# Hash-bucketed attention and a gated MLP on one core: the row maxima's last step as one reduction, running sums on GpSimd, a new planned order

## The chip, the cores and the metric

The kernel runs on one core of one Trainium2 chip. Times are microseconds of device time for one execution. The kernel before took a median of 816.7 us in three runs (815.85 to 816.98). TensorE is the matrix engine, VectorE, ScalarE and GpSimd the three elementwise engines (DVE, ACT and POOL in the profile), SyncE (SP) issues most transfers.

## The reference

```python
def attention(q, k, v, proj):                # (4, 8, 768, 64) each, proj (64, 6)
    q_bucket = bits(q @ proj > 0)            # 6 signs make a bucket number
    k_bucket = bits(k @ proj > 0)
    mask = q_bucket[..., :, None] == k_bucket[..., None, :]
    scores = where(mask, q @ k.T / sqrt(64), -1e9)
    scores = scores - max(scores, axis=-1)
    attn = exp(scores) / (sum(exp(scores), axis=-1) + 1e-9)
    return attn @ v

def mlp(x, w_in, g_ln, w_sg, b_sg, w_out):   # x: (4, 768, 512), the 8 heads side by side
    u, v = split(gelu_tanh(x @ w_in), 2)     # 512 columns each
    v_n = (v - mean(v)) / sqrt(var(v) + 1e-6) * g_ln
    v_s = w_sg @ v_n + b_sg[:, None]         # mixes the 768 positions
    return x + (u * v_s) @ w_out
```

## The kernel before

The attention works through 16 pairs of heads (`NPAIR`), the two heads of a pair on the two halves of the 128 partitions. For precision a matrix is split into a high and a low part, and products of parts are added in PSUM.

For a pair: `load` fetches q, k and v (SP queue). `parts` transposes q and k on TensorE (L494), ScalarE writes the high part (L498), VectorE the low part (L501). `features` multiplies by the projection (L514) and VectorE turns the results into signs (L519); the signs, scaled, go into extra rows of a matmul, so that scores of unequal buckets become very negative. `largest` computes approximate scores row by row (L539), and VectorE takes their negated maxima (L547 for a row of 512 keys, L549 for the last 256 keys of two rows at once). A pair has nine such units: three for the first 256 queries (phase 0) and six for the other 512 (phase 1). After the last unit of a phase `shift` joins the two parts of the maxima: L558 takes the minimum of the negated parts, L559 replaces values of empty rows by zero and writes the result into a zeroed tile `m`; TensorE spreads `m` into rows (L565), and ScalarE copies two rows into the feature tile (L571), where they become the shift that the scores get.

`weigh` computes the shifted scores with four matmul parts (L593), ScalarE exponentiates them into a tile `p` (L598), and an add joins `p` to a running sum a head (L620). `ADDS` names the engine of each add: GpSimd for all but the third of the five in phase 1. Every three units TensorE multiplies `p` by v (L608 and L611). `finish` adds the sums over partitions (L640), sends them through DRAM to get them into another layout (L649 to L655), takes the reciprocal (L651) and multiplies (GpSimd L662, then VectorE L663) before the result is written to DRAM.

Between all this VectorE and GpSimd convert the MLP's input weights: 16 weight jobs of seven VectorE operations (L363, L364, L366, L368, L369, L370, L372), one on GpSimd (L365) and one on ScalarE (L371).

The MLP then runs over 4 batches of 768 positions. `hidden` makes both halves (L806, L834), `gate` mixes the positions (L852, then VectorE L855, L859), `project` multiplies by w_out and adds x (L878, L883). For batch 0 the mixing weights are transposed first (L772, L778, L781), and the output weights converted by eight more weight jobs.

All instructions of both parts are handed to `Plan`, each with an engine, a cost in us, a due time (`prio`), what it reads and writes, and `port=True` where it is held to exclude GpSimd from VectorE. `Plan.order` runs a list schedule with these costs: an engine takes, of what is ready in the plan, what is due first; on TensorE a change of the kind of matmul adds `STAY` to the due time. The order that comes out is the order of the program on each engine; on the chip each engine works strictly in that order and waits on semaphores. Due times are in units of half a `weigh` unit: unit g is due at 2g, its totals at 2g + `FINP`, its products at 2g + `AVP`, the maxima of unit i at 2(i - `AHEAD`) + `S0P`, the preparation of the next pair at `PREP` against its start, weight job i at `WSTEP` i + `WP`. The MLP's due times begin at 480 and so lie behind all of the attention. PSUM has 7 banks for the attention's matmuls and one for the products; 16 `p` tiles are shared.

Of the kernel before, what the change touches and what calls it, by code (L numbers as in the profile page):

```python
# [18 lines left out]
DRAM = bass.MemoryType.DRAM  # L19


MLP = {"xl": "POOL", "gm": "DVE", "gl": "POOL", "wg": 209.05, "wo": 46.93, "x": 568.79}

AVP = 4.99
GY, GX, NPT = (1, 2), (3, 3), 16
NAV = 1
S0P = 2.08
AHEAD = 8
PREP, SHIFTP, FINP, WSTEP, WP = -3.85, 0.3, 6.08, 12.04, 25.31
LOADS = "SP"  # L30
ADDS = (["POOL", "POOL"], ["POOL", "POOL", "DVE", "POOL", "POOL"])
TAILP = 0.0


class Plan:
# [8 lines left out]
    TURNS = {"row": 0.2, "col": 0.144, "full": 0.17, "c32": 0.1, None: 0.0}  # L44
    LANES = 8
    TURN = 4.7
    STAY = 2.0

    class Buf:
        def __init__(self, make, i, prev, need=None):  # L50
# [178 lines left out]
def kernel(  # L229
# [99 lines left out]
    CW = 256  # L329
    wjobs = [(w_in, c, f0, CW, wih, wil, 1.0) for f0 in range(0, FF, CW) for c in range(NC)]  # L330

    def weight_job(plan, tile_of, src, c, f0, CW, th, tl, fac, prio):
        def part(t):
            return (t() if isinstance(t, Plan.Buf) else t)[:, c, f0:f0 + CW]

        bufs = [(t, (c, f0)) for t in (th, tl) if isinstance(t, Plan.Buf)]
        w = tile_of([P, CW, 2], I32, "w64")
        x, y = tile_of([P, CW], I32, "wx"), tile_of([P, CW], I32, "wy")
        g = tile_of([P, CW], F32, "wg")
        d = plan.buf("wd", 1000)  # L340
        V = nc.vector
        sts = V.scalar_tensor_tensor

        def load():
            nc.sync.dma_start(w().rearrange("p a b -> p (a b)"), src[c * P:(c + 1) * P, f0:f0 + CW].bitcast(I32))

        ops = iter(range(1, 12))

        def when():
            i = next(ops)  # L350
            return prio

        def vec(fn, r, wr):
            plan.add("DVE", 0.07 + CW / 960.0, when(), fn, r, wr, port=True)

        def vec2(fn, r, wr):
            plan.add("DVE", 0.07 + CW / 1920.0, when(), fn, r, wr, port=True)
# [4 lines left out]
        xf, yf = (lambda: x().bitcast(F32)), (lambda: y().bitcast(F32))  # L362
        vec2(lambda: V.tensor_scalar(y(), hi(), 3, 0x3FFFFFFF, op0=ALU.logical_shift_left, op1=ALU.bitwise_and), [w], [y])  # L363
        vec(lambda: sts(x(), hi(), -0x40000000, y(), op0=ALU.bitwise_and, op1=ALU.bitwise_or), [w, y], [x])  # L364
        plan.add("POOL", 0.14 + CW / 512, when(), lambda: nc.gpsimd.tensor_mul(g(), hi().bitcast(F32), hi().bitcast(F32)), [w], [g])  # L365
        vec(lambda: sts(xf(), g(), LEAST * LEAST, xf(), op0=ALU.is_ge, op1=ALU.mult), [x, g], [x])  # L366

        vec2(lambda: V.tensor_single_scalar(y(), x(), -0x800000, op=ALU.bitwise_and), [x], [y])  # L368
        vec(lambda: sts(yf(), lo().bitcast(U32), 2.0 ** -52, yf(), op0=ALU.mult, op1=ALU.mult), [w, y], [y])  # L369
        vec(lambda: V.tensor_add(xf(), xf(), yf()), [x, y], [x])  # L370
        plan.add("ACT", 0.06 + CW / 1300, when(), lambda: nc.scalar.mul(part(th), xf(), fac), [x], [d] + bufs[:1])  # L371
        vec(lambda: sts(part(tl), xf(), fac, part(th).bitcast(F32), op0=ALU.mult, op1=ALU.subtract),  # L372
            [x, d] + bufs[:1], bufs[1:])
# [50 lines left out]
    if True:  # L424
# [82 lines left out]
        def features(st, i, prio):  # L507
            hh, lo, ft, (_, cs, keys), fp = st.hi, st.lo, st.ft, chunk(i), ps_tile()
            n = cs.stop - cs.start

            def project():
                for c, (s, _) in enumerate(keys):
                    for u, (w, x) in enumerate(((pwh, hh), (pwl, hh), (pwh, lo))):
                        nc.tensor.matmul(fp()[:, c * n:(c + 1) * n], w[:, s, :], x()[:, s, cs], start=(u == 0), stop=(u == 2))  # L514

            plan.add(PE, 0.7, prio, project, [(t, x) for t in (hh, lo, ft) for x in keys], [fp], form="full")
            for c, (s, ph) in enumerate(keys):
                def sign(c=c, s=s):
                    nc.vector.tensor_scalar(ft()[:, s, cs], fp()[:, c * n:(c + 1) * n], fcol[:, 2 * s:2 * s + 1],  # L519
                                            fcol[:, 2 * s + 1:2 * s + 2], op0=ALU.is_gt, op1=ALU.mult)  # L520

                plan.add(DVE, 0.28 + n / 960.0, prio, sign, [fp], [(ft, (s, ph))])

        def largest(st, u, prio):

            ph = 0 if u < 3 else 1
            i, w = divmod(u - 3 * ph, 3)
            if u in (0, 3):
                st.mx = late.ring([P, 2, WIDE // P, 2], F32, "mx", 3)
            mx, sc, i0 = st.mx, [ps_tile() for j in range(2)], 2 * i  # L530
            (a, b), t0 = ((0, WIDE) if w < 2 else (WIDE, S)), PHASES[ph][0] // P + i0
            tiles = (w,) if w < 2 else (0, 1)

            def mm():
                for c, t in enumerate(tiles):
                    qs = slice((t0 + t) * P, (t0 + t + 1) * P)
                    for n, x in enumerate((st.ft, st.hi)):
                        for j in range(2):
                            nc.tensor.matmul(sc[j]()[:, c * NY:c * NY + b - a], x()[row(j), 0, qs], x()[row(j), 1, a:b],  # L539
                                             start=(n == 0), stop=(n == 1))  # L540

            plan.add(PE, 0.464, prio, mm, [(x, (0, ph)) for x in (st.hi, st.ft)] + [(x, (1, c)) for x in (st.hi, st.ft) for c in ((0, 1) if w < 2 else (1,))],
                     sc, form="row")
# [29 lines left out]
        def weigh(st, c, prio):  # L573
# [22 lines left out]
            plan.add(PE, 0.93, prio, mm, [(x, (0, ph)) for x in (hi, lo, ft)] + [(x, (1, y)) for x in (hi, lo, ft) for y in need], sc, form="row")  # L596
# [4 lines left out]
            if u + 1 in ends:  # L601
# [12 lines left out]
                plan.add(PE, 0.865 * len(us), prio + AVP, product, [t for x in us for t in ps[x]] + [st.v], [av], form="col")  # L614
            if u:
                e = ADDS[ph][u - 1]
                for j in range(2):
                    def add(j=j, e=e, first=st.p[0][j] if u == 1 else sums[j]):
                        a = first()[:, :, :NY] if u == 1 else two(first())
                        (nc.gpsimd if e == POOL else nc.vector).tensor_add(two(sums[j]()), a, p[j]()[:, :, :NY])  # L620

                    plan.add(e, 1.35 if e == POOL else 0.62, prio + 0.6, add, [p[j]] + ([st.p[0][j]] if u == 1 else []),
                             [sums[j]], port=True)

        def finish(st, ph, prio):
# [31 lines left out]
            if ph == 0:  # L657
# [277 lines left out]
```

## Time and profile before

| | us |
|---|---|
| median of three runs | 816.7 |
| the profiled execution | 820.94 |
| its span, first to last instruction | 818.8 |
| TensorE busy | 782.7 (96%) |
| VectorE busy | 539.0 (66%) |
| ScalarE busy | 359.6 (44%) |
| GpSimd busy | 370.6 (45%) |
| mean granted TensorE clock | 0.987 of full |

The busy shares are means over an attention part (to some 494 us) and an MLP part. A busy TensorE is not one at its peak: matmuls overlap, and their ends are modelled. The profile's chain of waits goes through TensorE for 74% of the span and through VectorE for 19%.

### The profile page before, as it was taken

The numbers are of one execution on the slowest core, as the hardware profiler recorded it, in microseconds if no ns is written. First come the engines' busy times: TensorE is split into PE (matmuls) and PEld (weight loads), VectorE is DVE, ScalarE is ACT, GpSimd is POOL, SyncE is SP. The second block draws the span as 40 slices with busy tenths as digits, with TensorE's granted clock in tenths as the row PEclk, the third lists the DMA queues.
The fourth block names the chain that finished last, engine by engine and source line by source line (L and its number), as shares of the span: only waits on it lengthen the run. The fifth ranks groups of instructions, "written<-read, shape, count | busy, mean of one in ns | idle before, by whom it ended". The sixth has DMA issues, their size and how long they took to land.

```text
span 818.8 us, 14669 instructions
## 1 busy us (share of the span) xinstructions
PE 782.7 (96%) x5608; PEld 599.2 (73%) x5608; DVE 539.0 (66%) x962; ACT 359.6 (44%) x703; POOL 370.6 (45%) x334
## 2 busy tenths in 40 slices
PE   6999998999999899998999999999999999999998
PEld 4767566657557566665767556988899889988996
DVE  7898987997988898897678644699323141405130
ACT  2556653646546454654656574532332123213211
POOL 0376664666556464663756676344006112401030
PEclk9999998999999999999999999999999999999999
DMA  5233232232232143232230123631402220131003
GB/s 129 52 86 73 66 98 58 68 98 73 64 100 60 65 104 73 60 92 52 54 98 21 54 78 118 218 98 39 129 27 78 82 73 6 34 124 31 1 1 128
DMA packets 98533, 60.63 MB, mean 74 GB/s; under 512 B 64672, under 2 KB 85280, under 8 KB 98464
## 3 DMA queue, kind: packets, MB, share of 16 engines
q1 hardware_dynamic: 96768, 56.94, 25.0%
q10 hardware_dynamic: 1696, 2.76, 1.0%
q8 instruction: 44, 0.72, 0.4%
q14 instruction: 25, 0.20, 0.1%
HBM read 46.90 MB, written 12.78 MB: 73 GB/s over the span
## 4 chain that ended last, share of the span: by engine, by line
PE 74%; DVE 19%; DMA 2%; issue 2%; ACT 2%; SPq 0%; POOL 0%; ACTq 0%; DVEq 0%
PE g L593 14%; PE ps_vs L852 11%; PE ps_o L878 8%; PE g L539 7%; PE av L608 7%; PE ps_h L806 7%; PE ps_h L834 6%; PE g L514 4%; PE av L611 4%; PE g L494 3%; DVE m L559 3%; DVE mx L547 2%; DVE mx L549 2%; DVE mx L558 2%; DVE xt L663 1%
## 5 line engine op out<-in xcount | busy, mean ns | idle before, releaser
L598 ACT ACTIVATE p<-g 128x512 f32<-128x512 f32 x288 | 155.7, 600 | 102.5 <-PE g L593 101.7
L620 POOL TENSOR_TENSOR sum<-sum,p 128x512 f32<-128x512 f32 x128 | 159.3, 1264 | 55.9 <-DVE sum L620 32.0
L547 DVE TENSOR_REDUCE mx<-g 128x1 f32<-128x512 f32 x192 | 121.7, 679 | 21.3 <-PE g L539 18.6
L620 POOL TENSOR_TENSOR sum<-p,p 128x512 f32<-128x512 f32 x64 | 85.4, 1354 | 87.4 <-ACT p L598 87.4
L608 PE MATMUL av<-p,v 128*64 128x512 f32 x384 | 89.6, 602 | 0.0
L593 PE MATMUL g<-h 64*128 64x256 f32 (+1 forms) x384 | 76.3, 360 | 5.6 <-DVE mx L547 4.9
L549 DVE TENSOR_REDUCE mx<-g 128x2 f32<-128x512 f32 x96 | 61.9, 684 | 23.9 <-PE g L539 22.0
L539 PE MATMUL g<-f 64*128 64x256 f32 (+1 forms) x384 | 73.2, 366 | 0.8 <-DVE f L519 0.5
L855 DVE SCALAR_TENSOR_TENSOR gt<-ps_vs,g_col,b_bc 128x384 f32<-128x384 f32 x32 | 19.7, 616 | 80.3 <-PE ps_vs L852 80.3
L593 PE MATMUL g<-h,l 64*128 64x256 f32 (+1 forms) x384 | 72.1, 342 | 0.0
L593 PE MATMUL g<-l,h 64*128 64x256 f32 (+1 forms) x384 | 71.0, 339 | 0.0
L593 PE MATMUL g<-f 64*128 64x256 f32 (+1 forms) x384 | 70.9, 338 | 0.0
L539 PE MATMUL g<-h 64*128 64x256 f32 (+1 forms) x384 | 68.3, 342 | 0.0
L863 POOL TENSOR_TENSOR gs<-gt,gs 128x384 fp32r<-128x384 f32 x32 | 32.8, 1026 | 74.0 <-ACT gs L860 74.0
L878 PE MATMUL ps_o<-woh,gs 128*128 128x512 f32 x192 | 65.5, 402 | 0.0
L852 PE MATMUL ps_vs<-wgh,zh 128*128 128x384 f32 x192 | 64.3, 335 | 0.6 <-DVE gt L855 0.6
L852 PE MATMUL ps_vs<-wgh,zl 128*128 128x384 f32 x192 | 64.2, 334 | 0.0
L852 PE MATMUL ps_vs<-wgl,zh 128*128 128x384 f32 x192 | 64.2, 334 | 0.0
L817 POOL TENSOR_TENSOR mv<-mv,epsr 128x1 f32<-128x1 f32 x24 | 15.6, 651 | 100.8 <-DVE mv L816 100.8
L593 PEld LDWEIGHTS g<-h 64*128 64x128 f32 x384 | 41.4, 186 | 26.8 <-DVE mx L547 8.8
L814 DVE BATCH_NORM_STATS2 st<-y 128x6 f32<-128x512 f32 x24 | 16.6, 690 | 64.0 <-ACT y L795 64.0
L608 PEld LDWEIGHTS av<-p,v 128*64 128x64 f32 x384 | 24.9, 137 | 43.8 <-issue 41.8
(118 smaller groups left out, 1754.1 us busy)
## 6 DMA issues: line engine op xcount, KB each, us to landing
q<-in_q_dram SPq DMA_DIRECT2D x32, 192.0 KB
k<-in_k_dram SPq DMA_DIRECT2D x32, 192.0 KB
v<-in_v_dram SPq DMA_DIRECT2D x16, 384.0 KB
x<-xs SPq DMA_DIRECT2D x16, 384.0 KB
rx<-xs SPq DMA_DIRECT2D x96, 64.0 KB
out_dram<-ob SPq DMA_DIRECT2D x24, 256.0 KB
w<-in_moe_w_in_dram SPq DMA_DIRECT2D x16, 256.0 KB
rs<-r SPq DMA_DIRECT2D x32, 128.0 KB
```

What stands on the lines that cost most here:

```text
L539: nc.tensor.matmul(sc[j]()[:, c * NY:c * NY + b - a], x()[row(j), 0, qs], x()[row(j), 1, a:b], start=(n == 0), stop=(n == 1))
L547: nc.vector.tensor_reduce(mx()[:, 0, i0 + w, j:j + 1], sc[j]()[:, :WIDE], axis=AX.X, op=ALU.max, negate=True)
L549: nc.vector.tensor_reduce(mx()[:, 1, i0:i0 + 2, j], two(sc[j]()), axis=AX.X, op=ALU.max, negate=True)
L593: nc.tensor.matmul(sc[j]()[:, i * w:(i + 1) * w], x()[row(j), 1, ks], y()[row(j), 0, cs], start=(m == 0), stop=(m == 3))
L598: plan.add(ACT, 0.6, prio, lambda j=j: nc.scalar.activation(p[j]()[:, :, :NY], two(sc[j]()), AF.Exp, scale=SCALE), [sc[j]], [p[j]])
L608: nc.tensor.matmul(two(av())[row(j)], st.v()[:, j, x, :], ps[x][j]()[:, :, :NY], start=(x == 0), stop=(x == 5))
L620: (nc.gpsimd if e == POOL else nc.vector).tensor_add(two(sums[j]()), a, p[j]()[:, :, :NY])
L806: nc.tensor.matmul(ps(), x()[:, ts_], w[:, c, FH:FF], start=(c == 0 and n == 0), stop=(c == NC - 1 and n == 2))
L834: nc.tensor.matmul(ps()[:, :SH], w[:, c, fs], x()[:, cs], start=(c == 0 and n == 0), stop=(c == NC - 1 and n == 2))
L852: nc.tensor.matmul(vp(), z()[:, t, fs], w()[:, t, cs], start=(t == 0 and n == 0), stop=(t == NT - 1 and n == 2))
L863: nc.gpsimd if e == POOL else nc.vector).tensor_sub(gl()[:, cs], gt(), gh()[:, cs].bitcast(F32)),
L878: nc.tensor.matmul(po(), a()[:, ts_], w()[:, f, :], start=(f == 0 and n == 0), stop=False)
```

## The change

The two operations L558 and L559 become one tensor_reduce. The tile of the maxima gets a third part that holds the constant `EMPTY` and is set once at the start, in three fixed tiles that are used in turn; the reduction takes the minimum over the three parts and writes into `m`. A row without a match now has `EMPTY` as its shift instead of zero. The one add of a pair's phase that ran on VectorE goes to GpSimd, for both heads. Costs and due times of the plan are changed, and L663 is no longer marked as excluding GpSimd. The weight job gets a `bank` argument with a second form of its operations; the callers don't pass it.

```diff
-MLP = {"xl": "POOL", "gm": "DVE", "gl": "POOL", "wg": 209.05, "wo": 46.93, "x": 568.79}
+MLP = {"xl": "POOL", "gm": "DVE", "gl": "POOL", "wg": 105.79, "wo": 112.68, "x": 652.19}
-AVP = 4.99
+AVP = 5.2
-S0P = 2.08
+S0P = 1.57
-PREP, SHIFTP, FINP, WSTEP, WP = -3.85, 0.3, 6.08, 12.04, 25.31
+PREP, SHIFTP, FINP, WSTEP, WP = -4.32, 0.3, 2.81, 14.6, 25.31
-ADDS = (["POOL", "POOL"], ["POOL", "POOL", "DVE", "POOL", "POOL"])
-TAILP = 0.0
+ADDS = (["POOL", "POOL"], ["POOL", "POOL", "POOL", "POOL", "POOL"])
+TAILP = 1.27
+WHURRY = 20.0
...
-    STAY = 2.0
+    STAY = 2.64
...
-    def weight_job(plan, tile_of, src, c, f0, CW, th, tl, fac, prio):
+    def weight_job(plan, tile_of, src, c, f0, CW, th, tl, fac, prio, bank=None):
...
+        mxs = [late.pool.tile([P, 3, WIDE // P, 2], F32, tag=f"mx{i}", name=f"mx{i}", bufs=1) for i in range(3)]
+        for t in mxs:
+            nc.vector.memset(t, EMPTY)
...
-            plan.add(PE, 0.7, prio, project, ...
+            plan.add(PE, 0.72 if i == 0 else 0.67, prio, project, ...
...
-                st.mx = late.ring([P, 2, WIDE // P, 2], F32, "mx", 3)
+                st.mx = plan.buf("mx", 3, lambda i: mxs[i % 3])
...
-            plan.add(PE, 0.464, prio, mm, ...
+            plan.add(PE, 0.45 if w < 2 else 0.48, prio, mm, ...
...
-            plan.add(DVE, 0.16, prio, lambda: V.tensor_tensor(mx()[:, 0, :nt], mx()[:, 0, :nt], mx()[:, 1, :nt], op=ALU.min), [mx], [mx], port=True)
-            plan.add(DVE, 0.16, prio, lambda: V.scalar_tensor_tensor(
-                m()[:, :nt, MROW::BL], mx()[:, 0, :nt], EMPTY, mx()[:, 0, :nt], op0=ALU.is_lt, op1=ALU.mult),
-                     [mx], [m], port=True)
+            plan.add(DVE, 0.18, prio, lambda: V.tensor_reduce(
+                m()[:, :nt, MROW::BL], mx()[:, :, :nt].rearrange("p a i j -> p i j a"), axis=AX.X, op=ALU.min), [mx], [m])
...
-            plan.add(PE, 0.93, prio, mm, ...
+            plan.add(PE, (0.96, 0.9)[ph], prio, mm, ...
...
-                plan.add(PE, 0.865 * len(us), prio + AVP, product, ...
+                plan.add(PE, 0.86 * len(us), prio + AVP, product, ...
...
-                    plan.add(e, 1.35 if e == POOL else 0.62, prio + 0.6, add, ...
+                    plan.add(e, 1.29 if e == POOL else 0.62, prio + 0.6, add, ...
...
-            plan.add(DVE, 0.1 + n / 960.0, prio + TAILP, lambda: V.scalar_tensor_tensor(
-                xt()[:, :n], e()[:, :n], vm()[:, 0:1], xt()[:, :n], op0=ALU.mult, op1=ALU.add), [xt, e, vm], [xt], port=True)
+            plan.add(DVE, 0.15 + n / 960.0, prio + TAILP, lambda: V.scalar_tensor_tensor(
+                xt()[:, :n], e()[:, :n], vm()[:, 0:1], xt()[:, :n], op0=ALU.mult, op1=ALU.add), [xt, e, vm], [xt])
```

## Rows read from the trace of the kernel before

**Rows 1.** Windows by stage; columns: length, busy of each engine, clock, DMA share, GB/s
```profile
41.10:437.40 396.30, 375.02 (x3200) 249.73 (x3200) 342.64 (x557) 214.25 (x433) 236.67 (x199) 0.97 0.29 74
437.40:494.20 56.80, 55.79 (x477) 33.91 (x476) 33.60 (x54) 34.51 (x68) 40.71 (x34) 1.00 0.19 55
494.20:593.50 99.30, 96.33 (x494) 85.99 (x495) 68.75 (x139) 37.24 (x71) 36.43 (x36) 1.00 0.39 124
593.50:659.50 66.00, 66.00 (x358) 61.70 (x358) 15.22 (x26) 16.89 (x30) 16.75 (x14) 1.00 0.23 72
659.50:737.30 77.80, 77.80 (x409) 71.26 (x408) 23.38 (x46) 21.77 (x38) 19.58 (x18) 1.00 0.17 52
```
**Rows 2.** Windows by pair: PE, PEld, DVE, ACT, POOL busy as in rows 1
```profile
41.10:69.50 28.40, 28.14 (x248) 18.57 (x247) 25.50 (x44) 16.46 (x35) 19.81 (x19) 1.00 0.29 72
191.20:221.50 30.30, 28.69 (x249) 18.81 (x249) 28.06 (x48) 17.40 (x37) 19.57 (x17) 1.00 0.28 75
381.40:408.70 27.30, 27.30 (x245) 18.34 (x246) 19.46 (x33) 15.11 (x31) 16.70 (x14) 1.00 0.29 75
```
**Rows 3.** Chain: by line from 381.4 to 408.7; pieces (start, us) from 98.6 to 131.3
```profile
by line: PE g L593 32.6%; PE av L608 20.0%; PE g L539 17.3%; PE av L611 10.1%; PE g L514 8.5%; PE g L494 5.3%; PE g L640 4.2%; PE g L565 2.2%
...
113.72 1.12 DVE m L559
...
115.07 1.34 DVE wx L364
```
**Rows 4.** Windows around a gap of TensorE, columns as in rows 1
```profile
120.00:128.40 8.40, 5.67 (x59) 3.63 (x55) 8.16 (x13) 4.45 (x11) 5.62 (x5) 0.97 0.06 19
128.40:131.30 2.90, 2.90 (x16) 2.39 (x17) 1.88 (x4) 1.09 (x2) 0.00 (x0) 0.50 0.05 2
```
**Rows 5.** Waits of TensorE from 41.1 to 437.4: us in total, times, longest
```profile
PE g L565 <- DVE m L559: 15.1, 15, 2.5
```
**Rows 6.** VectorE's groups from 41.1 to 437.4: busy us, mean ns, idle before
```profile
L559 DVE SCALAR_TENSOR_TENSOR m<-mx 128x8 fp32r<-128x8 f32 (+1 forms) x26 | 26.6, 1024 | 0.9
...
L663 DVE SCALAR_TENSOR_TENSOR xt<-e,vm,xt 128x256 f32<-128x256 f32 (+1 forms) x25 | 18.2, 729 | 0.0
L558 DVE TENSOR_TENSOR mx<-mx 128x8 f32<-128x8 f32 (+1 forms) x26 | 18.2, 700 | 0.5
L620 DVE TENSOR_TENSOR sum<-sum,p 128x512 f32<-128x512 f32 x26 | 17.7, 720 | 0.0
L372 DVE SCALAR_TENSOR_TENSOR wil<-wx,wih 128x256 fp32r<-128x256 f32 x16 | 14.0, 877 | 1.7 <-ACT wih L371 1.7
...
L368 DVE TENSOR_SCALAR wy<-wx 128x256 int32<-128x256 int32 x15 | 6.1, 407 | 0.4
```
**Rows 7.** Views of lines L559 and L651: min/median/max ns over the whole span
```profile
L559 DVE SCALAR_TENSOR_TENSOR m<-mx x32: 155/1108/1228, 18.1 to 474.4; 128x4 fp32r<-128x4 f32 x16, 128x8 fp32r<-128x8 f32 x16
...
L651 DVE RECIPROCAL sq<-sq x32: 160/182/203, 39.2 to 501.0; 128x4 f32<-128x4 f32 x16, 128x8 f32<-128x8 f32 x16
```
**Rows 8.** Timeline of GpSimd and VectorE, 177 to 181 us: start, us, instruction
```profile
177.39 2.78 POOL L620 TENSOR_TENSOR sum<-sum,p 128x512 f32<-128x512 f32 x2
...
179.09 1.11 DVE L559 SCALAR_TENSOR_TENSOR m<-mx 128x8 fp32r<-128x8 f32 x1
180.12 0.28 DVE L363 TENSOR_SCALAR wy<-w 128x256 int32<-128x256 int32 x1
...
180.90 0.42 DVE L366 SCALAR_TENSOR_TENSOR wx<-wg,wx 128x256 f32<-128x256 f32 x1
```
**Rows 9.** GpSimd's groups from 41.1 to 437.4, columns as in rows 6
```profile
L620 POOL TENSOR_TENSOR sum<-sum,p 128x512 f32<-128x512 f32 x106 | 132.4, 1267 | 47.0 <-DVE sum L620 30.1 <-ACT p L598 16.8
```
**Rows 10.** Timeline of GpSimd and TensorE, 171 to 179 us: last adds, then their total
```profile
171.38 2.42 POOL L620 TENSOR_TENSOR sum<-sum,p 128x512 f32<-128x512 f32 x2
...
178.17 0.64 PE L640 MATMUL g<-sum,ones 128*32 128x256 f32 x8
```

More of the change, by code (lines that the diff above doesn't have):

```diff
@@ L337, in weight_job @@
         w = tile_of([P, CW, 2], I32, "w64")
-        x, y = tile_of([P, CW], I32, "wx"), tile_of([P, CW], I32, "wy")
+        if bank is None:
+            bx, by = tile_of([P, CW], I32, "wx"), tile_of([P, CW], I32, "wy")
+            x, y, xk, yk, y2, y2k = bx, by, bx, by, by, by
+        else:
+            t = bank()
+            x, y = (lambda: t()[:, :CW].bitcast(I32)), (lambda: t()[:, CW:2 * CW].bitcast(I32))
+            y2 = tile_of([P, CW], I32, "wy")
+            xk, yk, y2k = (t, 0), (t, 1), y2
         g = tile_of([P, CW], F32, "wg")
@@ L350, in when @@
             i = next(ops)
-            return prio
+            return prio if bank is None or i == 1 else prio - WHURRY
         def vec(fn, r, wr):
-            plan.add("DVE", 0.07 + CW / 960.0, when(), fn, r, wr, port=True)
+            plan.add("DVE", (0.07 if bank is None else 0.14) + CW / 960.0, when(), fn, r, wr, port=bank is None)
         def vec2(fn, r, wr):
-            plan.add("DVE", 0.07 + CW / 1920.0, when(), fn, r, wr, port=True)
+            plan.add("DVE", 0.07 + CW / 1920.0 if bank is None else 0.14 + CW / 960.0, when(), fn, r, wr, port=bank is None)
@@ L359, in weight_job @@
         lo, hi = (lambda: w()[:, :, 0]), (lambda: w()[:, :, 1])
         plan.add("SP", 0.55, prio - 2, load, [], [w], dma=0.73 * CW / 256)
-        xf, yf = (lambda: x().bitcast(F32)), (lambda: y().bitcast(F32))
-        vec2(lambda: V.tensor_scalar(y(), hi(), 3, 0x3FFFFFFF, op0=ALU.logical_shift_left, op1=ALU.bitwise_and), [w], [y])
-        vec(lambda: sts(x(), hi(), -0x40000000, y(), op0=ALU.bitwise_and, op1=ALU.bitwise_or), [w, y], [x])
+        xf, yf, zf = (lambda: x().bitcast(F32)), (lambda: y().bitcast(F32)), (lambda: y2().bitcast(F32))
@@ L365, in weight_job @@
+        vec2(lambda: V.tensor_scalar(y(), hi(), 3, 0x3FFFFFFF, op0=ALU.logical_shift_left, op1=ALU.bitwise_and), [w], [yk])
+        vec(lambda: sts(x(), hi(), -0x40000000, y(), op0=ALU.bitwise_and, op1=ALU.bitwise_or), [w, yk], [xk])
         plan.add("POOL", 0.14 + CW / 512, when(), lambda: nc.gpsimd.tensor_mul(g(), hi().bitcast(F32), hi().bitcast(F32)), [w], [g])
-        vec(lambda: sts(xf(), g(), LEAST * LEAST, xf(), op0=ALU.is_ge, op1=ALU.mult), [x, g], [x])
-        vec2(lambda: V.tensor_single_scalar(y(), x(), -0x800000, op=ALU.bitwise_and), [x], [y])
@@ L369, in weight_job @@
-        vec(lambda: sts(yf(), lo().bitcast(U32), 2.0 ** -52, yf(), op0=ALU.mult, op1=ALU.mult), [w, y], [y])
-        vec(lambda: V.tensor_add(xf(), xf(), yf()), [x, y], [x])
-        plan.add("ACT", 0.06 + CW / 1300, when(), lambda: nc.scalar.mul(part(th), xf(), fac), [x], [d] + bufs[:1])
+        vec(lambda: sts(xf(), g(), LEAST * LEAST, xf(), op0=ALU.is_ge, op1=ALU.mult), [xk, g], [xk])
+        vec2(lambda: V.tensor_single_scalar(y(), x(), -0x800000, op=ALU.bitwise_and), [xk], [yk])
+        vec(lambda: sts(zf(), lo().bitcast(U32), 2.0 ** -52, yf(), op0=ALU.mult, op1=ALU.mult), [w, yk], [y2k])
@@ L372, in weight_job @@
+        vec(lambda: V.tensor_add(xf(), xf(), zf()), [xk, y2k], [xk])
+        plan.add("ACT", 0.06 + CW / 1300, when(), lambda: nc.scalar.mul(part(th), xf(), fac), [xk], [d] + bufs[:1])
         vec(lambda: sts(part(tl), xf(), fac, part(th).bitcast(F32), op0=ALU.mult, op1=ALU.subtract),
-            [x, d] + bufs[:1], bufs[1:])
+            [xk, d] + bufs[:1], bufs[1:])
     PE, DVE, ACT, POOL, SP = "PE", "DVE", "ACT", "POOL", "SP"
@@ L514, in project @@
                         nc.tensor.matmul(fp()[:, c * n:(c + 1) * n], w[:, s, :], x()[:, s, cs], start=(u == 0), stop=(u == 2))
-            plan.add(PE, 0.7, prio, project, [(t, x) for t in (hh, lo, ft) for x in keys], [fp], form="full")
+            plan.add(PE, 0.72 if i == 0 else 0.67, prio, project, [(t, x) for t in (hh, lo, ft) for x in keys], [fp], form="full")
             for c, (s, ph) in enumerate(keys):
@@ L540, in mm @@
                                              start=(n == 0), stop=(n == 1))
-            plan.add(PE, 0.464, prio, mm, [(x, (0, ph)) for x in (st.hi, st.ft)] + [(x, (1, c)) for x in (st.hi, st.ft) for c in ((0, 1) if w < 2 else (1,))],
+            plan.add(PE, 0.45 if w < 2 else 0.48, prio, mm, [(x, (0, ph)) for x in (st.hi, st.ft)] + [(x, (1, c)) for x in (st.hi, st.ft) for c in ((0, 1) if w < 2 else (1,))],
                      sc, form="row")
@@ L595, in weigh @@
             need = sorted({0 if kt * P < NY else 1 for kt in kts})
-            plan.add(PE, 0.93, prio, mm, [(x, (0, ph)) for x in (hi, lo, ft)] + [(x, (1, y)) for x in (hi, lo, ft) for y in need], sc, form="row")
+            plan.add(PE, (0.96, 0.9)[ph], prio, mm, [(x, (0, ph)) for x in (hi, lo, ft)] + [(x, (1, y)) for x in (hi, lo, ft) for y in need], sc, form="row")
             for j in range(2):
@@ L612, in product @@
                                                  start=(x == 0 and i == 0), stop=(x == 2 and i == 1))
-                plan.add(PE, 0.865 * len(us), prio + AVP, product, [t for x in us for t in ps[x]] + [st.v], [av], form="col")
+                plan.add(PE, 0.86 * len(us), prio + AVP, product, [t for x in us for t in ps[x]] + [st.v], [av], form="col")
             if u:
@@ L620, in add @@
                         (nc.gpsimd if e == POOL else nc.vector).tensor_add(two(sums[j]()), a, p[j]()[:, :, :NY])
-                    plan.add(e, 1.35 if e == POOL else 0.62, prio + 0.6, add, [p[j]] + ([st.p[0][j]] if u == 1 else []),
+                    plan.add(e, 1.29 if e == POOL else 0.62, prio + 0.6, add, [p[j]] + ([st.p[0][j]] if u == 1 else []),
                              [sums[j]], port=True)
```

## The prediction

> **What bounds the kernel now.** I read the busy time by stage first, then by pair of heads, then the chain of waits inside a good and a bad pair, then what TensorE waited for, and last the durations of the VectorE and GpSimd operations that the diff touches.
>
> The attention fills the first 494 us and the MLP the rest [rows 1]. Of the attention, the stretch from 41.1 to 437.4 us is regular: it starts and ends where the transposes for a next pair begin and holds 13 pairs, so a pair takes 396.3 / 13 = 30.48 us. In the MLP a steady batch has TensorE busy for all of its 77.8 us, so nothing that the change does to other engines can shorten it.
>
> The reader is to see two kinds of pair [rows 2]. The one from 381.4 to 408.7 us takes 27.3 us, TensorE has no gap in it, and its chain consists of TensorE lines alone [rows 3]: 27.33 us is what a pair costs when TensorE is the only limit. That pair has 19.5 us of VectorE work. The others carry more VectorE work (25.5 us, 28.1 us) and take longer (28.4 us, 30.3 us). In such a pair the chain leaves TensorE and runs through VectorE: the second half of the shift at L559 for 1.12 us, then a weight operation at L364 for 1.34 us [rows 3]. So the loss against TensorE alone is 396.3 - 13 x 27.33 = 41.0 us. Of it TensorE was idle 396.3 - 375.0 = 21.3 us [rows 1]; 15.1 us of that is the wait of the spreading matmul L565 for the shift [rows 5]. A clock loss follows the gaps: in a stretch in which TensorE worked 5.67 of 8.40 us the clock was still 0.97, and in the 2.90 us behind it 0.50, the lower of its two levels (1.2 GHz instead of 2.4) [rows 4]. The mean clock of 0.97 over the 396.3 us is some 10 to 12 us of the loss; the remainder is matmuls drawn out by late weights.
>
> **Why VectorE is late.** L558 and L559 work on 4 or 8 numbers a partition, yet L559 has a median of 1108 ns and a minimum of 155 ns [rows 7]. The timeline shows why: two GpSimd adds run from 177.39 to 180.17 us; L559 starts at 179.09 us and ends at 180.20 us, with the second add. Right behind it, with GpSimd free, weight operations take 0.28 and 0.42 us [rows 8]. A VectorE operation that reads two SBUF tensors waits here for the GpSimd add to end. RECIPROCAL at L651, which reads one SBUF tensor of the same size, takes 160 to 203 ns in all 32 cases [rows 7], although GpSimd is 60% busy: it doesn't wait.
>
> **The change, part by part** (sums for the 13 pairs, which hold 26 shifts).
>
> 1. The shift. Two operations (26.6 + 18.2 = 44.8 us [rows 6]) become one tensor_reduce over 24 or 12 numbers that reads one SBUF tensor. The trace has no tensor_reduce from SBUF. From below it costs 0.16 us, the fastest RECIPROCAL; from above 1.11 us, the median of L559, if it waits for GpSimd as that does. I take 0.18 us, near RECIPROCAL, since it too has a single SBUF input: 26 x 0.18 = 4.7 us. VectorE gains 40.1 us, and the way from the last maximum to the spreading matmul shrinks by 1.5 us each time.
> The Trainium skill ("SBUF — State Buffer", section "Who interferes with whom") says that on trn2 a tensor_reduce never contends with GpSimd, while an operation with two SBUF inputs does. By it the upper end falls away and the sum stays as it is; by that rule, L559 and L651 agree, but no row here shows the reduce itself.
>
> 2. The adds. Two of VectorE's adds a pair go to GpSimd: VectorE loses 17.7 us [rows 6], GpSimd gains 26 x 1.267 = 32.9 us [rows 9]. GpSimd goes from 236.7 us of 396.3 (60%) [rows 1] to 269.6 of some 363 (74%). It has the room. In the six-unit half of a pair it now has five double adds of 2.53 us in 6 x 27.33 / 9 = 18.2 us, so they cannot queue up without end.
>
> 3. What that does to the rest of VectorE. The weight operations stay: seven kinds, 67.3 us in all, from 14.0 (L372) to 6.1 us (L368) [rows 6]. At 0.28 us for two kinds and 0.42 us for five [rows 8], their 106 operations would take 40 us, so they wait 27 us, 0.25 us each. With GpSimd's share up by a quarter I add a quarter to that, and the same for L663: 8 us. At best this is nothing, at worst each of the 131 operations waits 1 us more (a whole add, as L559 does).
>
> 4. The order. Due times and the planner's costs move: the shift is now planned at 0.18 us and without GpSimd, the totals are due 3.27 units earlier (1.6 units of weighing), the weight jobs spread wider. Its effect is bounded below by 27.33 us a pair and above by today's mean of 30.48. The new branch of the weight job (a bank argument) is never taken, as no call passes one; it costs nothing. The three constant tiles cost three VectorE memsets at the start, under the first loads: nothing, and 0.2 us uncovered.
>
> 5. The MLP. Gate weights are now due ahead of the output weights, x loads later. Batches 0 and 1 take 99.3 + 66.0 = 165.3 us against 2 x 77.8 = 155.6: 9.7 us is the most to win, and part of it is transposes that stay. TensorE idles only 3.0 us of the 99.3 [rows 1], since matmuls of batch 1 fill in where weights are late. I take zero, between -9.7 and +10 us.
>
> **The sum.** VectorE's work falls from 342.6 us [rows 1] by 26.6 + 18.2 + 17.7, and rises by 4.7 + 8, to 292.8 us, 22.5 us a pair. The pairs at 19.46 and 25.5 us took 27.3 and 28.4 us [rows 2]; between them, 22.5 us gives 27.3 + 1.1 x 3.04 / 6.04 = 27.9 us. That is 13 x (30.48 - 27.9) = 33.6 us saved. The last two pairs (56.8 us [rows 1], against 27.33 + 27.1 at best) give 0.8 us; for the first 41 us I count nothing, as their maxima and loads are the same; the memsets cost 0.2 us. Together -34.2 us: the profiled execution goes from 820.94 to 786.7 us. The median of the runs stood at 816.7 / 820.94 = 0.9948 of it, which gives 783 us.
>
> **Rivals.**
> TensorE alone: every pair reaches 27.33 us, and the MLP gives 4 us. 41.0 + 2.4 + 4 = 47.4 us: 769 us. For it speaks that the cover left on VectorE is 4.8 us a pair, against it that weight operations still wait in bursts. Chance 0.13.
> The waits move: GpSimd, busy three quarters of the time, holds up the weight operations and L663 more than I add, so VectorE stays near 26 us a pair and a pair takes 29.3 us: 13 x 1.2 = 15.3 us saved, 801 us. Decided by whether L366 and its like go well over their present means. Chance 0.13.
> The reduce waits for GpSimd as L559 does: then only L558 and the adds are gone, and at L559's mean [rows 6] 26 x (1.02 - 0.18) = 21.8 us of VectorE work come back: 24.2 us a pair, 28.2 us by the same interpolation, and a shift that comes 0.84 us late twice with the clock loss behind it; I put a pair at 29.2 us, 800 us. Against it stands L651. Chance 0.04.
> The totals stall TensorE (the other side): L640, 32 times, needs GpSimd's last adds. Today the adds end at 173.80 us and L640 starts at 178.17 us, 4.4 us later [rows 10]; being due 1.6 units (4.9 us) earlier uses this slack up. If GpSimd then runs later than planned by one add, TensorE, which works in order, stands 1.27 us at each of 32 totals with the weighing matmuls queued behind: +40.6 us against -34.2, 823 us. It decides from 1.07 us a total. Against it: the planner still places a total only after its adds, with a cost of 1.29 us for an add that takes 1.27 us. Chance 0.10, part of it ending near no change.
>
> **How the numbers follow.** The forecast has 0.60 and by itself spans 27.4 to 28.6 us a pair, 776 to 792 us. The range goes from 769 (TensorE alone) to 803 us (waits moved, reduce waiting) and leaves out the stalled totals. A change under 0.2%, 1.6 us, can't be told from none. Faster 0.90 (the first four cases), within 0.2% 0.03, slower 0.07.
>
> **What would show it.** Right: the reduce at about 0.18 us without long cases; L565's wait for the shift nearly gone; TensorE idle under 10 us and clock 0.99 or more over 13 pairs of some 27.9 us; VectorE near 22.5 us and GpSimd near 20.7 us a pair. Wrong: a reduce that ends with GpSimd's adds, L640 waiting for sums by more than a few us in all, weight operations over twice their bare time, or an MLP stage for batch 0 and 1 far from 165 us.

## The result, and the profile after

The changed kernel takes 796.54 us (median of 4 executions, 789.33 to 796.78); the kernel before, beside it, 816.28 us (815.66 to 816.98). The ratio of the means is 0.9737, 95% interval 0.9681 to 0.9792. The forecast was 783 us with a range of 769 to 803. The profiled execution took 796.62 us with a span of 794.8 us, against 820.94 and 818.8 before.

The windows by stage of the changed kernel, with the columns of [rows 1]; the first line is the stretch ahead of the 13 regular pairs, the last two are a pair with weight jobs and one without:

```profile
0.00:42.60 42.60, 33.12 (x260) 23.73 (x260) 37.17 (x98) 16.23 (x32) 11.00 (x23) 1.00 0.37 93
42.60:406.70 364.10, 362.46 (x3198) 244.13 (x3198) 303.08 (x502) 211.15 (x429) 259.12 (x221) 1.00 0.31 81
406.70:470.70 64.00, 59.29 (x484) 36.33 (x482) 34.83 (x46) 34.47 (x68) 47.51 (x42) 0.95 0.15 45
470.70:558.50 87.80, 85.79 (x441) 77.41 (x440) 65.91 (x132) 35.44 (x66) 37.14 (x36) 1.00 0.36 110
558.50:635.60 77.10, 77.10 (x415) 70.31 (x414) 18.03 (x34) 20.06 (x36) 17.47 (x15) 1.00 0.30 95
99.60:128.10 28.50, 28.26 (x248) 18.83 (x247) 26.79 (x46) 16.68 (x36) 21.10 (x19) 1.00 0.34 89
351.90:379.30 27.40, 27.40 (x248) 18.74 (x246) 19.33 (x32) 15.95 (x33) 19.15 (x17) 1.00 0.29 74
```

The 24.0 us of span come from one place and are partly lost at another. The 13 pairs take 364.1 us instead of 396.3 (-32.2, 28.0 us a pair), with TensorE idle for 1.6 us and the clock at 1.00. The start is 1.5 us longer, the last two pairs 64.0 instead of 56.8 us (+7.2), and the MLP takes 324.1 instead of 324.6 us. The cut between these two stages isn't at quite the same event: the MLP's first matmul, before and then after, is

```profile
493.02 0.50 PE L806 MATMUL ps_h<-wih,xh 128*128 128x512 f32 x1
```
```profile
470.73 0.50 PE L815 MATMUL ps_h<-wih,xh 128*128 128x512 f32 x1
```

so the cut of [rows 1] at 494.2 us lies 1.2 us behind it. Counted from that matmul, the last two pairs are 8.3 us longer and the MLP is 1.7 us shorter.

The 32 us are not the same gain in every pair. Counted pair by pair, before, 11 of the 13 pairs hold weight operations and take 30.93 us on average, the other two 28.02. After, 7 pairs hold them and take 28.46, the other 6 take 27.48: the planned order now puts two jobs into each of fewer pairs (99 weight operations in the 13 pairs, before 106), and such a pair costs 1 us more than a bare one instead of 3.

VectorE's and GpSimd's groups over the 13 pairs, as in [rows 6] and [rows 9], and then two lines over the whole span as in [rows 7]:

```profile
L672 DVE SCALAR_TENSOR_TENSOR xt<-e,vm,xt 128x256 f32<-128x256 f32 (+1 forms) x25 | 38.6, 1543 | 13.4 <-POOL xt L671 13.4
L377 DVE SCALAR_TENSOR_TENSOR wy<-w,wy 128x256 f32<-128x256 uint32 x14 | 12.9, 924 | 0.5
L380 DVE SCALAR_TENSOR_TENSOR wil<-wx,wih 128x256 fp32r<-128x256 f32 x15 | 6.3, 420 | 2.6 <-ACT wih L379 2.6
L569 DVE TENSOR_REDUCE m<-mx 128x8 fp32r<-128x24 f32 (+1 forms) x26 | 4.6, 176 | 0.9
L629 POOL TENSOR_TENSOR sum<-sum,p 128x512 f32<-128x512 f32 x130 | 160.8, 1264 | 13.0 <-ACT p L607 13.0
```
```profile
L569 DVE TENSOR_REDUCE m<-mx x32: 168/176/186, 18.0 to 450.1; 128x4 fp32r<-128x12 f32 x16, 128x8 fp32r<-128x24 f32 x16
...
L672 DVE SCALAR_TENSOR_TENSOR xt<-e,vm,xt x32: 740/1420/8700, 60.5 to 489.7; 128x256 f32<-128x256 f32 x16, 128x512 f32<-128x512 f32 x16
```

The reduce is short in all 32 cases. The addition to x (L672; L663 before) went from 18.2 us for 25 [rows 6] to 38.6 us, and one of them took 8.70 us. The timeline around that one, GpSimd, VectorE and TensorE (start, us, engine, instruction, idle time before):

```profile
438.84 1.31 POOL L671 TENSOR_TENSOR xt<-un,rs 128x512 f32<-128x512 f32 x1
440.10 4.66 POOL L629 TENSOR_TENSOR sum<-sum,p 128x512 f32<-128x512 f32 x4
440.19 8.70 DVE L672 SCALAR_TENSOR_TENSOR xt<-e,vm,xt 128x512 f32<-128x512 f32 x1 [1.79 <-POOL xt L671]
444.68 2.52 POOL L629 TENSOR_TENSOR sum<-p,p 128x512 f32<-128x512 f32 x2
447.14 1.20 POOL L629 TENSOR_TENSOR sum<-sum,p 128x512 f32<-128x512 f32 x1
448.81 1.28 DVE L560 TENSOR_REDUCE mx<-g 128x2 f32<-128x512 f32 x2
450.12 0.18 DVE L569 TENSOR_REDUCE m<-mx 128x8 fp32r<-128x24 f32 x1
450.45 1.08 PE L574 MATMUL g<-identr,m 128*128 128x128 f32 x4 [4.46 <-DVE m L569]
```

L672 starts 0.09 us into the first of seven adds in a row, and ends only after the last of them has. The next maxima and the shift stand behind it on VectorE, so TensorE waits 4.46 us at L574, and from 430 to 470.3 us the clock averages 0.92. The wait and the clock behind it account for the lengthening of the last two pairs. The single execution at 789.33 us lies 7.2 us below the others; that fits an execution without this stall, but it has no trace.

### The profile page after: what moved, and what is told of

It reads as the page before. It is cut to its first block, busy times and chain, and to the rows that moved or that the text cites. A ratio compares the mean times of both kernels' runs of the same rounds, so it can differ in the third digit from the quotient of the medians.

```text
span 794.8 us, 14631 instructions
## 1 busy us (share of the span) xinstructions
PE 773.4 (97%) x5608; PEld 594.3 (75%) x5608; DVE 504.3 (63%) x901; ACT 358.3 (45%) x703; POOL 403.8 (51%) x366
## 4 chain that ended last, share of the span: by engine, by line
PE 84%; DVE 10%; ACT 2%; issue 1%; DMA 1%; POOL 1%; SPq 0%; POOLq 0%; DVEq 0%; ACTq 0%
PE g L602 14%; PE ps_vs L861 13%; PE av L617 9%; PE ps_h L843 8%; PE ps_o L887 8%; PE ps_h L815 8%; PE g L550 7%; PE av L620 4%; PE g L525 4%; PE g L505 3%; DVE mx L558 2%; PE g L649 2%; DVE mx L560 2%; DVE xt L672 2%; PE g L574 1%
## 5 line engine op out<-in xcount | busy, mean ns | idle before, releaser
L629 POOL TENSOR_TENSOR sum<-sum,p 128x512 f32<-128x512 f32 x160 | 196.7, 1257 | 14.7 <-ACT p L607 14.7
L558 DVE TENSOR_REDUCE mx<-g 128x1 f32<-128x512 f32 x192 | 123.6, 684 | 33.8 <-PE g L550 32.5
L629 POOL TENSOR_TENSOR sum<-p,p 128x512 f32<-128x512 f32 x64 | 82.0, 1298 | 118.7 <-ACT p L607 118.7
L550 PE MATMUL g<-f 64*128 64x256 f32 (+1 forms) x384 | 73.5, 353 | 3.2 <-DVE f L530 1.1
L672 DVE SCALAR_TENSOR_TENSOR xt<-e,vm,xt 128x256 f32<-128x256 f32 (+1 forms) x32 | 54.5, 1704 | 31.9 <-POOL xt L671 17.4
L602 PE MATMUL g<-h 64*128 64x256 f32 (+1 forms) x384 | 73.4, 361 | 0.1
L602 PE MATMUL g<-h,l 64*128 64x256 f32 (+1 forms) x384 | 68.4, 337 | 0.0
L550 PE MATMUL g<-h 64*128 64x256 f32 (+1 forms) x384 | 68.4, 337 | 0.0
L602 PE MATMUL g<-f 64*128 64x256 f32 (+1 forms) x384 | 68.1, 336 | 0.0
L602 PE MATMUL g<-l,h 64*128 64x256 f32 (+1 forms) x384 | 67.9, 335 | 0.0
L550 PEld LDWEIGHTS g<-f 64*128 64x128 f32 x384 | 41.1, 185 | 31.3 <-ACT f L580 15.1
```

Of the source, the lines that this page charges most:

```text
L672: plan.add(DVE, 0.15 + n / 960.0, prio + TAILP, lambda: V.scalar_tensor_tensor(xt()[:, :n], e()[:, :n], vm()[:, 0:1], xt()[:, :n], op0=ALU ...
```

## The experiments

All compare with the kernel before, run beside them; medians in us, ratios of means with their 95% intervals. The planner sets the order of work anew from each kernel's costs, so no edit leaves the order otherwise untouched. "Old plan" means the costs and due times of the kernel before, "new plan" those of the change.

**One part alone, old plan.** First the shift (the kernel before with `mx` of three parts and the reduce), then the adds, then both:

```diff
+ plan.add(DVE, 0.18, prio, lambda: V.tensor_reduce(m()[...], mx()[...].rearrange("p a i j -> p i j a"), axis=AX.X, op=ALU.min), [mx], [m])
```


> The kernel before with only the reduce in place of L558 and L559 (planned at 0.18 us, without port); adds, due times and all other costs as before. Theory A (the shift's wait for GpSimd was the loss): 302 us of VectorE work over the 13 pairs, pairs of about 28.2 us, 13 x 2.3 = 30 us saved: 787 us, range 782 to 795. Theory B (the new due times are what brings the pairs to 28 us, the reduce alone only moves the waits): 802 to 812 us.

```diff
- ADDS = (["POOL", "POOL"], ["POOL", "POOL", "DVE", "POOL", "POOL"])
+ ADDS = (["POOL", "POOL"], ["POOL", "POOL", "POOL", "POOL", "POOL"])
```


> The kernel before with only the third add of phase 1 moved to GpSimd. Theory A: L558 and L559 stay and wait for a GpSimd that is busier (66% instead of 60%), their mean rises from 0.70 and 1.02 us; VectorE has 17.7 us less to do but the shift is as late as before: 810 to 818 us. Theory C (the adds on VectorE were half of the loss): 795 to 805 us.

> The kernel before with the reduce and with all adds on GpSimd, but its old due times and costs. Theory B (the planned order decides; the waits for GpSimd move from the shift to the weight operations, whose 106 operations rose from 67 to 84 us with the reduce alone): 806 to 816 us, no better than the adds alone (811.8). Theory A (the shift's wait was the loss, and needed the room on VectorE as well): 788 to 796 us.

The reduce alone: 819.92, ratio 1.0032 (1.0005 to 1.0059). The adds alone: 811.83, 0.9936 (0.9911 to 0.9960). Both: 816.41, 0.9994 (0.9969 to 1.0019). The reduce alone lies above both expected ranges, the adds alone in theory A's, both together 0.4 us above theory B's. So the wait of the shift, which [rows 5] puts at 15.1 us, could be removed and nothing was won. The window over the 13 pairs of the first, and its weight operations (columns as in [rows 6]):

```profile
41.50:438.20 396.70, 378.95 (x3200) 251.38 (x3199) 325.28 (x536) 211.46 (x431) 236.83 (x197) 0.97 0.29 74
```
```profile
L364 DVE SCALAR_TENSOR_TENSOR wx<-w,wy 128x256 int32<-128x256 int32 x15 | 15.8, 1052 | 0.4
L368 DVE TENSOR_SCALAR wy<-wx 128x256 int32<-128x256 int32 x15 | 15.2, 1011 | 0.4
```

VectorE has 17 us less to do than in [rows 1], yet the pairs take as long. L368, 0.407 us before [rows 6], takes 1.01 us; the 106 weight operations take 84.0 us together instead of 67.3. The timeline of one job (VectorE, then GpSimd) shows how:

```profile
87.48 0.18 DVE L561 TENSOR_REDUCE m<-mx 128x8 fp32r<-128x24 f32 x1
89.14 1.40 DVE L364 SCALAR_TENSOR_TENSOR wx<-w,wy 128x256 int32<-128x256 int32 x1
90.57 1.29 DVE L366 SCALAR_TENSOR_TENSOR wx<-wg,wx 128x256 f32<-128x256 f32 x1
91.90 1.17 DVE L368 TENSOR_SCALAR wy<-wx 128x256 int32<-128x256 int32 x1
93.11 0.43 DVE L369 SCALAR_TENSOR_TENSOR wy<-w,wy 128x256 f32<-128x256 uint32 x1
```
```profile
88.88 1.37 POOL L621 TENSOR_TENSOR sum<-p,p 128x512 f32<-128x512 f32 x1
90.22 2.70 POOL L621 TENSOR_TENSOR sum<-sum,p 128x512 f32<-128x512 f32 x2
```

Each weight operation ends with an add, and the next waits through the next add: three cost 3.9 us while GpSimd adds, the fourth 0.43 us behind the adds. The row of adds takes the price from whatever VectorE holds at that moment. With the shift gone it is the weight job, and TensorE waits 16.4 us, in 11 waits, for maxima (L594 and L542) instead of for the shift; ahead of all but one of them VectorE has just worked through operations of a weight job.

**The new plan without one part or without both.** Without both; with the third add back on VectorE; with the two-operation shift back:

```diff
- ADDS = (["POOL", "POOL"], ["POOL", "POOL", "POOL", "POOL", "POOL"])
+ ADDS = (["POOL", "POOL"], ["POOL", "POOL", "DVE", "POOL", "POOL"])
...
+ plan.add(DVE, 0.16, prio, lambda: V.tensor_tensor(mx()[...], mx()[...], mx()[...], op=ALU.min), [mx], [mx], port=True)
+ plan.add(DVE, 0.16, prio, lambda: V.scalar_tensor_tensor(m()[...], mx()[...], EMPTY, mx()[...], op0=ALU.is_lt, op1=ALU.mult), [mx], [m], port=True)
```


> The changed kernel with the two-operation shift (planned at 0.16 us each with port, as before) and the third add on VectorE again: only the due times, STAY and the planner's other costs are new. Theory A: 808 to 820 us, within 1% of before. Theory B: 795 to 803 us.

> The changed kernel with the third add of phase 1 on VectorE again. Theory A: 24.0 us of VectorE work a pair, pairs of 28.1 us, and no row of seven GpSimd adds in the last pairs, so that no L672 takes over 3 us: 788 to 793 us, faster than the changed kernel's 796.5. Theory C: 800 to 808 us.

> The changed kernel with the shift as two operations again (planned at 0.16 us each, with port); adds on GpSimd, new due times and costs. Theory B: 796 to 804 us; the reduce is worth at most 1%. Theory A: 808 to 818 us.

Without both 802.64, ratio 0.9818 (0.9767 to 0.9868). Only the add back 803.20, 0.9829 (0.9769 to 0.9889). Only the shift back 826.30, 1.0134 (1.0089 to 1.0179): slower than before, and outside both expected ranges. Without both lies in theory B's range, the add back in theory C's. So the plan alone holds some 14 of the 20 us, and the other two parts together 6. Against the one execution of the changed kernel that took 789.33 us, without the stall by its time, the 6 would be some 13; the trace without both parts has no such stall (its longest L671 takes 2.30 us). One by one the parts give something else: the reduce alone, put on the new plan, wins nothing (803.20 against 802.64), and the adds alone cost 24 us. The chain in the kernel with the adds alone on the new plan, VectorE with ScalarE, then GpSimd:

```profile
121.86 1.43 DVE L372 SCALAR_TENSOR_TENSOR wx<-w,wy 128x256 int32<-128x256 int32 x1
123.40 1.19 DVE L374 SCALAR_TENSOR_TENSOR wx<-wg,wx 128x256 f32<-128x256 f32 x1
...
126.29 0.42 DVE L378 TENSOR_TENSOR wx<-wx,wy 128x256 f32<-128x256 f32 x1
126.74 0.42 ACT L379 ACTIVATE wih<-wx 128x256 fp32r<-128x256 f32 x1 [4.55 <-DVE wx L378]
127.06 0.57 ACT L654 COPY un<-av 128x512 f32<-128x512 f32 x1
122.94 2.70 POOL L628 TENSOR_TENSOR sum<-sum,p 128x512 f32<-128x512 f32 x2
```
```profile
PE av L619 <- ACT un L654: 19.6, 8, 2.6
```
```profile
127.60:131.00 3.40, 3.31 (x14) 1.92 (x16) 3.33 (x9) 1.07 (x3) 0.61 (x1) 0.50 0.72 221
```

Here the job is late for ScalarE: L379 waits 4.55 us, the copy `un` stands behind it in ScalarE's queue, and TensorE needs `un` to free its accumulator: 8 waits, 19.6 us, and behind this one 3.4 us at the lower clock (0.50). Pairs with weight jobs take 32.51 us in this kernel, the others 28.0.

**Is it the weight operations alone?** In these two kernels the seven VectorE operations of each input-weight job are issued as reduces over groups of one, which read one tensor; the plan and its costs stay. The conversion of the input weights is left out by that.

```diff
+ def one(to, frm, real):
+     if src is not w_in: return real()
+     V.tensor_reduce(to, frm.rearrange("p (a b) -> p a b", b=1), axis=AX.X, op=ALU.max)
```


> The kernel with the reduce alone (819.9 us), its plan and order unchanged, but each of the seven VectorE operations of an input-weight job is issued as a tensor_reduce over groups of one, of the same 256 columns, with a single SBUF input; this leaves out the conversion of w_in. Theory G (the weight operations, planned at 0.34 us, wait for a GpSimd add each in bursts of five to six, and the bursts hold up the next maximum and ScalarE's queue): no weight operation over 0.6 us, all pairs near 28.0 us as those without weight jobs, 13 pairs about 366 us: 786 to 796 us. Theory H (the order itself is bad, whatever the operations take): 808 to 820 us.

> The same replacement in the changed kernel with the shift as two operations (826.3 us), order unchanged; it leaves out the conversion of w_in. Theory G: pairs fall from 32.4 to about 28.2 us, 786 to 798 us, within 1.5% of the same replacement in the kernel with the reduce alone, though 826.3 and 819.9 lie on both sides of before. Theory H: 812 to 827 us.

On the reduce alone (0.1 us under theory G's range): 785.89, ratio 0.9616 (0.9578 to 0.9655), 34 us below the same plan with the real operations. On the new plan with the two-operation shift (in theory G's range): 794.85, 0.9728 (0.9694 to 0.9762), 31 us below. The windows over the 13 pairs of the two:

```profile
41.30:402.80 361.50, 361.22 (x3201) 242.41 (x3199) 286.19 (x535) 211.33 (x431) 230.43 (x197) 1.00 0.32 82
```
```profile
41.80:405.30 363.50, 362.84 (x3201) 242.75 (x3199) 297.22 (x534) 211.92 (x432) 255.49 (x224) 1.00 0.32 82
```

In the first the 106 weight operations now take 0.424 us on average and 0.529 at most, pairs with a job 27.74 and without 27.96 us, and TensorE idles 0.3 us. That is the clearest verdict of these runs: where nothing in a weight job waits for GpSimd, even the old plan leaves TensorE next to no idle time. The old plan's 13 pairs (361.5 us) are then no longer than the new plan's (363.5 us), which points to the weight operations' meetings with adds as what sets the plans apart.

**Weight jobs out of the way in a kernel that computes the reference.** The job's middle results in PSUM, through the change's unused `bank` argument (with the edit of the next paragraph). The argument also makes most operations of a job due 20 units earlier (`WHURRY`) and plans those on VectorE at other costs and without `port`, so the order is another one too:

```diff
- weight_job(plan, w_tile, *job, WSTEP * i + WP)
+ weight_job(plan, w_tile, *job, WSTEP * i + WP, bank=ps_tile)
```


> The changed kernel with the last pair's third add on VectorE (786.4 us), and with ps_tile passed as bank to the input-weight jobs: x and y of a job lie in a PSUM bank, so that each of its VectorE operations reads one SBUF tensor at most; the whole computation is kept. Theory G: the 1.05 us that pairs with weight jobs cost more than those without goes: 775 to 783 us. Rival: one of the seven banks is missing for the scores while a job holds it, and TensorE waits for a bank: 788 to 805 us.

792.07, ratio 0.9709 (0.9664 to 0.9755). Its profiled execution is the long one (797.76) and has a stall of 8.7 us like the one below; the other three took 791.8 to 792.1. The weight operations do fall (means of 0.42 to 0.47 us a kind), but pairs with a job take 28.9 us, not less than the 28.46 of the changed kernel: theory G's range is missed. The rival's range, for a PSUM bank that TensorE then misses, holds, but not its mechanism as far as the trace tells: TensorE idles 1.7 us in the 13 pairs and no wait names a bank. What costs the time here, the bank, the earlier due times or the order, stays open.

**The stall of 8.70 us.** First, the last pair's third add back on VectorE; then GpSimd and VectorE alone, 96 trials of one multiply and eight adds against one L672, computing nothing of the reference; then half of `xt` reduced ahead of L672, so that L672 asks later:

```diff
+ e = "DVE" if st.n == NPAIR - 1 and ph == 1 and u == 3 else ADDS[ph][u - 1]
```


> The changed kernel, only the third add of phase 1 of the last pair on VectorE instead of GpSimd. In the changed kernel's profile one L672 waited 8.7 us, through seven adds that GpSimd ran without a gap, and the MLP began 7 us late. Theory S (a VectorE operation with two SBUF inputs can lose the port to a row of adds until the row ends): the row is cut, no L672 over 3.5 us, 787 to 791 us in all runs. Theory T (the long wait has another cause, such as the transfers of the totals): 795 to 797 us still.

> Leaves out the whole computation: 96 trials of one multiplication and eight adds of 128x512 in a row on GpSimd, and one scalar_tensor_tensor of 128x512 on VectorE that is released by the multiplication, so that it arrives 0.1 us after the first add has begun, or up to 0.6 us later behind a reduction of 1 to 497 numbers. In the first half the adds read tiles that ScalarE writes anew for each trial. Theory S: most VectorE operations wait for one add (1.1 to 1.7 us), some for two to eight (up to 10 us), and the arrival decides which. Theory T: all take 1.1 to 1.7 us.

```diff
+ V.tensor_reduce(top, xt()[:, :n // 2], axis=AX.X, op=ALU.max)
  V.scalar_tensor_tensor(xt()[:, :n], e()[:, :n], vm()[:, 0:1], xt()[:, :n], ...)
```


> The changed kernel, its plan unchanged; VectorE takes the maximum of half of each xt tile (a tensor_reduce with one SBUF input) right ahead of L672, so that L672 asks for its second operand 0.3 us later into GpSimd's add. In the changed kernel L672 asked 0.10 us after an add had begun and waited through seven; three of its four executions took 796.5 us, one 789.3. Theory U (the lock-out needs a request just after an add has begun, in a row of adds): no L672 over 3 us, all executions 788 to 792 us. Theory V (any request into that row can be locked out): an L672 of 8 us or executions of 795 to 798 us among the six.

The first gave 786.43, ratio 0.9649 (0.9608 to 0.9689), the best version that computes the reference, 10 us below the changed kernel. It doesn't settle the cause, and neither theory's range holds: five of its six executions took 786.2 to 787.0, and the profiled one, at 794.44, has the stall all the same, as the row belongs to the pair ahead of the edit. So most of the 10 us is how often the stall comes: with the stall on both sides the edit is worth 2.2 us (794.44 against 796.62), without it 2.9 us (786.4 against 789.33, by their times), and the two kernels weren't run beside each other. Why the stall comes in one execution and not in the next is not known; here and with the middle results in PSUM only the profiled one is long, in the changed kernel two of the three others are too. The line:

```profile
440.84 8.71 DVE L672 SCALAR_TENSOR_TENSOR xt<-e,vm,xt 128x512 f32<-128x512 f32 x1 [1.79 <-POOL xt L671]
```

In the second (1050.8 us in all), 95 of the 96 operations waited for the add that they met and for no other (0.95 to 1.66 us, as theory T has it but for the shortest), 31 of them from 67 to 83 ns into it. The 96th, 97 ns into an add, took 0.63 us, and that add took 1.76 us instead of 1.17. One of the 95, with its GpSimd row:

```profile
565.96 5.02 POOL L68 TENSOR_TENSOR sum<-sum,p 128x512 f32<-128x512 f32 x4
...
566.47 1.21 DVE L71 SCALAR_TENSOR_TENSOR xt<-e,vm,xt 128x512 f32<-128x512 f32 x1
```

So a row of adds by itself didn't lock VectorE out in any of the 96 trials. The third took 790.10 (789.24 to 790.72), 0.9693 (0.9667 to 0.9719), with the 13 pairs as in the changed kernel and no long L672 in its trace:

```profile
L675 DVE SCALAR_TENSOR_TENSOR xt<-e,vm,xt x32: 751/1032/2301, 62.0 to 483.6; 128x256 f32<-128x256 f32 x16, 128x512 f32<-128x512 f32 x16
```

The operation in the place of the long one, with its GpSimd row, of which it waits for the first add alone:

```profile
440.86 5.09 POOL L630 TENSOR_TENSOR sum<-sum,p 128x512 f32<-128x512 f32 x4
```
```profile
441.46 1.15 DVE L675 SCALAR_TENSOR_TENSOR xt<-e,vm,xt 128x512 f32<-128x512 f32 x1
```

Its MLP starts at 464.06 us, against 470.73 in the changed kernel, and all five executions lie within 1.5 us: asked for later, the seven adds were not waited through in the trace, and by their times not in the other executions. (The interval overlaps that of the changed kernel, which has one execution without the stall; the trace carries this verdict.) That is theory U's range. But a late request is no safeguard: three of its L675 operations, the longest of 2.30 us among them, asked 0.58 to 0.60 us into an add and still waited through the next one too, to the end of a row of two. What makes VectorE wait for a whole row stays open.

## Why the prediction came out as it did

The range held the time and the sign was right; the reasoning was right in part. 796.54 us lies above the 776 to 792 us that the forecast by itself spanned; the range held it because its rivals stretch it to 803. Only the one execution at 789.33 us lies within the forecast's own span.

**The shift (step 1)** was right: 26 x 0.176 = 4.6 us, forecast 4.7, and L565's wait is gone. The reduce takes 168 to 186 ns in all 32 cases with GpSimd busy 71% of the time, as RECIPROCAL did; the rule quoted from the Trainium skill ("SBUF — State Buffer", "Who interferes with whom") agrees with that. What the step took from it was wrong: it called the shift's wait 15.1 us of the loss, and the reduce alone wins nothing.

**The adds (step 2)**: GpSimd 259.1 us, 71%, forecast 269.6 and 74%; right.

**The rest of VectorE (step 3)**: forecast +8 us. L672 alone rose by 20.4 us, while 99 weight operations took 59.5 us instead of 106 taking 67.3; VectorE stands at 303.1, not 292.8. The step spread the waits evenly, a quarter of a microsecond each. In fact they come in bursts, at 1.2 to 1.4 us an operation while a row of adds runs.

**The order (step 4)** was only bounded, between 27.33 and 30.48 us a pair, and the sum then left it out. The runs show it to be the largest part, 14 us of 20 without the other two. The step also read the larger `WSTEP` as weight jobs that "spread wider"; the trace shows the opposite, 7 of the 13 pairs hold them instead of 11.

**The sum's interpolation** gave 27.9 us a pair and 28.0 was measured, but by a rule that doesn't hold, so the agreement is luck. VectorE's busy time doesn't set the pair: the reduce alone and the adds alone have 325.3 and 326.7 us of it and take 396.7 and 381.6 us; the new plan with the two-operation shift has 316.3 us and takes 400.0, the one without both parts 318.4 and takes 375.2. The windows of the last two:

```profile
41.60:441.60 400.00, 380.37 (x3200) 251.94 (x3198) 316.34 (x534) 212.69 (x432) 261.64 (x224) 0.95 0.29 74
```
```profile
41.90:417.10 375.20, 365.58 (x3200) 243.30 (x3198) 318.35 (x560) 211.98 (x432) 230.09 (x197) 1.00 0.30 79
```

What sets it, by the traces, is which operations meet a row of adds, and who is queued behind them.

**The failing step** is "the last two pairs give 0.8 us": they cost 7.2, for the stall of L672, which the prediction didn't see. The 8.0 us between, with 1.4 us in the pairs, 1.3 at the start and -0.5 in the MLP, are the difference between the forecast's 34.2 and the span's 24.0 us. The rest of the miss, some 3.7 us, is the factor 0.9948 from the profiled execution to the median: before, the profiled one was long; after, it is the median (796.62 and 796.54).

**The MLP (step 5)**: batches 0 and 1 take 87.8 + 77.1 = 164.9 us, before 165.3 (166.5 from the first matmul on); zero was right within that.

**The rivals.** "The waits move" named the mechanism that decides, but it happens in kernels with only a part of the change (the reduce alone, with L366 at 1.00 us against 0.74, and both on the old plan); in the changed kernel L374, the same operation, takes 0.51 us, and two others of a job rise (L377, 0.92 against 0.63 us, and L378, 0.85 against 0.58). "The totals stall TensorE" is refuted: the matmuls of L649 wait for sums 0.2 us in the whole attention. "The reduce waits" is refuted. "TensorE alone" is nearly there in the 6 pairs without jobs (27.48 us) and stands 1 us off in the 7 with jobs.

## What to carry to other kernels

When an operation waits for a resource in a trace, ask who will meet that resource once it no longer waits: here the wait moved from the shift to the weight jobs, and removing it alone won nothing. Read waits by what they meet (a row of adds, a burst of weight operations, a queue behind them), not as a busy sum to be spread over all operations. A plan prices operations at bare durations, 0.34 us for most weight operations here, while beside a row of the other engine's adds one took 1.2 to 1.4 us; charging that price is worth a trial, which no run here made. And one part of such a change may well be a loss without the others.

## What was not expected of the hardware

A VectorE operation of the L672 kind that meets a running GpSimd add normally waits for that one add: 95 of 96 cases in the kernel of those two engines. The Trainium skill ("SBUF — State Buffer", "Summary: rules for kernel authors") has it so too: of a VectorE operation with two SBUF inputs and a GpSimd operation that reads SBUF, the second to issue is blocked until the first has finished. In the 96th case the add, though begun first, was the one that took longer. Yet over the traces of all kernels here 11 operations, all of the L672 kind, waited until a whole row of GpSimd operations had ended, through two to seven of them and up to 8.71 us. Eight had begun 68 to 98 ns after a GpSimd operation, the other three are those of the kernel that asks later. Other operations began at the same offsets and waited for one add only, so the offset doesn't decide it alone.

L368 reads a single SBUF tensor, and it waited for adds all the same (1.17 us in the timeline above, 0.407 on average before [rows 6]). The prediction took two SBUF inputs to be what waits; that is too narrow. RECIPROCAL and the reduces from SBUF, also with one input, took no such time in any trace: at most 0.21 us for RECIPROCAL, 0.19 for the shift's reduce, 0.56 for a weight operation issued as a reduce.
